# Agent attention and a maxout network in one kernel: one pool of PSUM banks, output products in two shapes, eleven more query groups turned by DMA, and a new order of all work

## The chip, the cores and the metric

The kernel runs on one core of a Trainium2 chip. Its time is the device time of one execution in microseconds (us); three runs of the kernel before gave 451.64, 454.34 and 454.73, median 454.34.

## The reference

Attention goes through 49 agents per batch; then each row passes a network whose hidden layer is the maximum of three products.

```python
B, N, C = (4, 12544, 128); n_agents = 49          # q, k, v: B x N x C, float32
def sm(a, b):                                      # softmax of scale * a @ b.T over b's rows
    ...
a2k = sm(agents, k)
agent_v = a2k @ v                                  # 49 x 128 per batch
q2a = sm(q, agents)
x = q2a @ agent_v                                  # 50176 rows of 128
h = max(max(x @ w1, x @ w2), x @ w3)               # 768 wide
out = h @ w_out                                    # 50176 x 128, float32
```

## The kernel before, in words

**Algebra.** Since x is q2a times a 49 x 128 matrix, the kernel multiplies the weights into that matrix once per batch (G, 49 agents by 1792 columns, kept twice, in partitions 0 to 48 and 64 to 112). With e the unnormalised exponentials of a query group, the hidden layer is e times parts of G. The maximum of three is written as w1 + max(0, w3 - w1, w2 - w1): two hidden products (u with the columns of w3 - w1, v with those of w2 - w1), a ReLU and a maximum, and a linear product for w1, which goes into the output bank directly (L582, out_linear). The row's sum divides at the very end.

**Stages.** Keys and values come in chunks of nine times 128 rows, cast to bf16. Batch 0 is done first: its chunks are transposed on PE (L342), scored (L359), exponentiated, summed (L370) and multiplied with the values (L376). Batches 1 to 3 follow beside the query work: their chunks are transposed by a DMA that SP issues (L454, tile KT<-KB).

**Query groups.** There are 49 groups s of 1024 rows, 12 per batch, and a last one with 256 rows of each batch. Per group: load, cast on POOL (L517), eight 128 x 128 transposes on PE into PSUM (L523) and a copy on DVE (L527), or, for groups 38 to 48 (TURNED), a DMA transposition from SP (L454, tile QT<-QB). Then scores (L533), exponentials on ACT (L539), sums (L545) and reciprocals (L550). The group's 1024 rows stand as two halves of 64 partitions side by side, so that each hidden product is a pair of matmuls of 49 rows and 512 columns in the two halves of the PE array (L558). For each of six blocks f of 128 hidden columns: u on PE, ReLU on ACT (L571), v on PE, maximum on DVE (L574) into the tile R; for f = 4 ACT does it in place and out of place (L565, L568) while v adds to u in PSUM. Output: 48 matmuls of R with w_out (L592, out_hidden) and four linear ones (L582), 0.5 group per output bank, each bank scaled by the reciprocals on DVE (L599) and the group stored.

**Forms on PE.** PE works in three forms: all 128 rows; two row halves (the hidden products); two column halves (scores, G). 

**PSUM.** Eight banks: three fixed pairs (UV, for u, v and the wide tiles) and two single banks (OM, for outputs, scores, sums and turned queries).

**Order.** All instructions of all engines stand in one hand-written list (ORDER); a name in it is one step of the function graph, and the number behind the slash is the slot that its new tile takes. The framework sets the waits by the tiles that are read and written. On each engine, and in SP's DMA queue, work runs strictly in this order. `Plan.add` holds a cost with each step; nothing in the kernel reads it.

Of the kernel before, what the change touches and what calls it, by code (L numbers as in the profile page):

```python
# [9 lines left out]
FP32 = mybir.dt.float32  # L10
# [7 lines left out]
DFF = NF * P  # L18
SCALE = 1.0 / math.sqrt(C)
C31, C21, C1O, WC = 0, DFF, 2 * DFF, 2 * DFF + 2 * C  # L20
CV, CS, CT = KT * A, KT * A + A, (KT - 1) * A
# [4 lines left out]
TURNED = range(38, 49)  # L26
# [5 lines left out]
SLOTS = {"UV": 3, "OM": 2, "LD": 13, "QB": 3, "KB": 3, "VB": 4, "KT": 3, "QT": 3, "EQ": 4, "EK": 4, "AS": 3,  # L32
         "R": 13, "RC": 4, "OS": 9, "G": 4, "VA": 2, "EA": 2, "ES": 2, "KR": 2}
SHAPE = {"UV": ([P, 2, 512], FP32), "OM": ([P, 512], FP32), "LD": ([P, KT, C], FP32), "QB": ([P, GT, C], BF16),
# [6 lines left out]
class Plan:  # L41


    def __init__(self):
        self.ops, self.index, self.tiles, self.maker = [], {}, {}, {}

    def add(self, name, eng, fn, cost, mode=FULL, after=(), new=(), use=(), bank=None, serve=0.0):
        self.index[name] = len(self.ops)
        for cls, t in new:
            self.tiles[t] = cls  # L50
            self.maker[t] = name
        seq = [self.maker[t] for t in use if self.maker[t] not in after]
        self.ops.append(dict(name=name, eng=eng, fn=fn, pace=cost[0], lat=cost[1], mode=mode, after=list(after), seq=seq,
                             new=[t for _, t in new], use=[t for _, t in new] + list(use), bank=bank, serve=serve))

    def places(self, order, given):

        left = {}
        for o in self.ops:
            for t in o["use"]:  # L60
                left[t] = left.get(t, 0) + 1
        free = {c: list(range(n)) for c, n in SLOTS.items()}
        place = {}
        for name in order:
            o = self.ops[self.index[name]]
            for i, t in enumerate(o["new"]):
                slots = free[self.tiles[t]]
                place[t] = slots.pop(slots.index(given[name][i]) if name in given else 0)
            for t in o["use"]:
                left[t] -= 1  # L70
                if left[t] == 0:
                    free[self.tiles[t]].append(place[t])
        return place

# [20 lines left out]
def mm(n, cols):  # L95
    t = n * max(cols / 2400 + 0.0025, 0.0253)
    return t, t + 0.235
# [18 lines left out]
def graph(plan, em):  # L116
# [3 lines left out]
    add("prep", PE, em.prep, (0.3, 3.6))  # L120
    ch = chunks(0)
    for g, (t0, n) in enumerate(ch):
# [4 lines left out]
        add(f"kt0.{g}", PE, em.k_turn(g, n), mm(n, 128), after=[f"kc0.{g}", "prep"], new=[("UV", f"kT_ps0.{g}")], use=[f"kb0.{g}"])  # L127
        add(f"ke0.{g}", DVE, em.k_evacuate(g, n), dve_half(n * 128), after=[f"kt0.{g}"], new=[("KT", f"kT0.{g}")], use=[f"kT_ps0.{g}"])
        add(f"ks0.{g}", PE, em.k_scores(0, g, n, f"s0.{g}"), mm(n, 49), after=[f"ke0.{g}"], new=[("UV", f"s0.{g}")], use=[f"kT0.{g}"])
        add(f"kx0.{g}", ACT, em.k_exps(0, g, n, f"s0.{g}"), (n * 0.041 + 0.07, n * 0.041 + 0.2), after=[f"ks0.{g}"],  # L130
            new=[("EK", f"e0.{g}")], use=[f"s0.{g}"])
        add(f"to0.{g}", PE, em.totals(g, n), mm(1, n * 49), after=[f"kx0.{g}"], new=[("OM", "acc")] if g == 0 else [],
            use=[f"e0.{g}"] + (["acc"] if g else []))
# [8 lines left out]
    for g in range(SPARE):  # L142
        add(f"wm.{g}", PE, em.warm(g), (0.2225, 0.45), new=[("UV", f"warm.{g}")])
# [12 lines left out]
    add("tw1", PE, em.turn_w1, mm(NF, 128), after=["cw1", "prep"], new=[("OM", "tw1")])  # L156
    add("ew1", DVE, em.evacuate_w1, dve_half(DFF), after=["tw1"], use=["tw1"])
    add("cwo", POOL, em.cast_wo, (0.77, 0.85), after=["lwo"], use=["wo"])
    add("rc0", DVE, em.recip_first, (0.85, 0.97), after=[f"to0.{g}" for g in range(last + 1)], new=[("KR", "kr0")], use=["acc"])
# [3 lines left out]
    for name, c, d, eng in (("a", C31, ["d31a"], ACT), ("b", C31 + half, ["d31b", "d32"], DVE), ("c", C21, ["d21a"], ACT),  # L163
                            ("d", C21 + half, ["d21b"], DVE)):
        add(f"gp{name}", PE, em.product(0, c, c + half, f"gp{name}"), mm(1, half), mode=COL, after=["nr0"] + d, new=[("UV", f"gp{name}")])
        add(f"gv{name}", eng, em.product_out(0, c, c + half, c, f"gp{name}", eng), act(half) if eng == ACT else dve(half),
            after=[f"gp{name}"], use=[f"gp{name}", "G0"])
    add("pl", PE, em.prep_linear, mm(NF, 128), after=["ew1", "cwo"], new=[("OM", "pl")])
    add("el", ACT, em.evacuate_linear, (0.17, 0.31), after=["pl"], use=["pl"])
    add("gl", PE, em.product(0, C1O, WC, "gl"), mm(1, 256), mode=COL, after=["nr0", "el"], new=[("OM", "gl")])  # L170
    add("gvl", ACT, em.product_out(0, C1O, WC, C1O, "gl", ACT), act(256), after=["gl"], use=["gl", "G0"])


    hosting = set()
    for b in range(1, B):
        ch = chunks(b)
        for g, (t0, n) in enumerate(ch):
            r, m = f"{b}.{g}", f"m.{host_of(b, g)}"
            hosting.add(host_of(b, g))
# [7 lines left out]
            add(f"ks{r}", PE, em.k_scores(b, g, n, m), mm(n, 49), after=[f"kt{r}"], new=[("OM", m)], use=[f"kT{r}"], bank=m)  # L187
            add(f"kx{r}", ACT, em.k_exps(b, g, n, m), (n * 0.041 + 0.07, n * 0.041 + 0.2), after=[f"ks{r}"], new=[("EK", f"e{r}")],
                use=[m], bank=m)
            add(f"kv{r}", PE, em.values(b, g, n, m), mm(n, 49), after=[f"kx{r}", f"vc{r}"], use=[m, f"vb{r}", f"e{r}"], bank=m)  # L190
            add(f"va{r}", DVE, em.add_values(b, g, m), (0.13, 0.25), after=[f"kv{r}"] + ([f"va{b}.{g - 1}"] if g else []),
                new=[] if g else [("VA", f"va{b}")], use=[m] + ([f"va{b}"] if g else []), bank=m)
            if g < len(ch) - 1:
                add(f"ea{r}", POOL, em.add_exps(b, g), (0.97, 1.06), after=[f"kx{r}"] + ([f"ea{b}.{g - 1}"] if g else []),
                    new=[] if g else [("EA", f"ea{b}")], use=[f"e{r}"] + ([f"ea{b}"] if g else []))
        g = len(ch) - 1
        add(f"fo{b}", POOL, em.fold(b), (1.25, 1.35), after=[f"ea{b}.{g - 1}"], new=[("ES", f"es{b}")], use=[f"ea{b}"])
        add(f"to{b}", PE, em.total(b, g, n, m), (n * 0.0253 + 0.1, n * 0.0253 + 0.335), after=[f"fo{b}", f"kv{r}"],
            use=[m, f"es{b}", f"e{r}"], bank=m)
        add(f"nr{b}", DVE, em.normalise(b, m), (0.5, 0.62), after=[f"to{b}", f"va{r}"], new=[("KR", f"kr{b}"), ("G", f"G{b}")],  # L200
            use=[m, f"va{b}"], bank=m)
        for name, c0, c1, eng in (("a", C31, C31 + DFF, ACT), ("c", C21, C21 + DFF, DVE), ("l", C1O, WC, ACT)):
            w = c1 - c0
            add(f"gp{name}{b}", PE, em.product(b, c0, c1, f"gp{name}{b}"), mm(1, w), mode=COL, after=[f"nr{b}", "el"],
                new=[("UV" if w > 512 else "OM", f"gp{name}{b}")])
# [4 lines left out]
    for s in range(NQ):  # L210
        parts = parts_of(s)
# [6 lines left out]
        else:  # L218
            add(f"qt.{s}", PE, em.q_turn(s), mm(GT, 128), after=[f"qc.{s}", "prep"], new=[("OM", f"qT_ps.{s}")], use=[f"qb.{s}"])
            add(f"qe.{s}", DVE, em.q_evacuate(s), (0.636, 0.735), after=[f"qt.{s}"], new=[("QT", f"qT.{s}")], use=[f"qT_ps.{s}"])  # L220
        add(f"sc.{s}", PE, em.q_scores(s), mm(len(parts), 512 // len(parts)), mode=COL, after=[f"qd.{s}" if s in TURNED else f"qe.{s}"],
            new=[("OM", f"qs.{s}")], use=[f"qT.{s}"])
        add(f"ex.{s}", ACT, em.q_exps(s), (0.56, 0.65), after=[f"sc.{s}"], new=[("EQ", f"e.{s}")], use=[f"qs.{s}"])
        m = f"m.{s}"
        h = s in hosting
        add(f"su.{s}", PE, em.sums(s, m, not h), mm(GT // 2, 2), after=[f"ex.{s}"] + ([f"ks{b}.{g}" for b in range(1, B)
            for g in range(len(LATER)) if host_of(b, g) == s] if h else []), new=[] if h else [("OM", m)], use=[f"e.{s}"] + ([m] if h else []),
            bank=m)
        add(f"re.{s}", DVE, em.recips(s, m), (0.13, 0.25), after=[f"su.{s}"], new=[("RC", f"rc.{s}")], use=[m], bank=m)
        for f in range(NF):  # L230
            def needs(base, first, second):
# [29 lines left out]
class Emit:  # L261
    def __init__(self, nc, pools, io):
# [10 lines left out]
        for t in self.avT:  # L273
            nc.vector.memset(t, 0.0)
# [590 lines left out]
```

## Time and profile before

| | us |
|---|---|
| median of three runs | 454.34 (451.64 to 454.73) |
| profiled execution, span from first to last instruction | 449.8 |
| PE busy (weight loads beside it) | 423.7 (274.0) |
| DVE busy | 402.8 |
| ACT busy | 395.1 |
| POOL busy | 169.4 |
| DMA moved | 117.8 MB |

Of the profiled execution the span is what is given; the runs' times hold what lies around it, too. Busy times are unions of the instructions' spans. On PE they include the pipeline's depth, so that matmuls overlap in the trace, and a price of one is better read from start to start. A line L558 is a line of the kernel; the two sides of `<-` are the tiles that it writes and reads. PEld is the weight load, SPq the issuing of DMAs by SP.

### The profile page before, as it was taken

The numbers are of one execution on the slowest core, as the hardware profiler recorded it, in microseconds if no ns is written. First come the engines' busy times: TensorE is split into PE (matmuls) and PEld (weight loads), VectorE is DVE, ScalarE is ACT, GpSimd is POOL, SyncE is SP. The second block draws the span as 40 slices with busy tenths as digits, with TensorE's granted clock in tenths as the row PEclk, the third lists the DMA queues.
The fourth block names the chain that finished last, engine by engine and source line by source line (L and its number), as shares of the span: only waits on it lengthen the run. The fifth ranks groups of instructions, "written<-read, shape, count | busy, mean of one in ns | idle before, by whom it ended". The sixth has DMA issues, their size and how long they took to land.

```text
span 449.8 us, 13103 instructions
## 1 busy us (share of the span) xinstructions
PE 423.7 (94%) x5388; PEld 274.0 (61%) x5388; DVE 402.8 (90%) x512; ACT 395.1 (88%) x461; POOL 169.4 (38%) x176
## 2 busy tenths in 40 slices
PE   0778899999999999999999999999999999999996
PEld 0654466666665666666666666666666655565675
DVE  1335999999999999999999999999999999999986
ACT  1459999999988999999989999999889899999983
POOL 1641645455676372464363263453402110100000
PEclk9989999999999999999999999999999999999999
DMA  8999999999999998999969799498608685327142
GB/s 311 409 408 387 326 373 310 263 394 316 340 320 274 392 216 223 408 273 318 406 200 324 216 350 226 141 314 336 212 6 230 191 221 129 96 103 178 48 177 107
DMA packets 80150, 117.80 MB, mean 262 GB/s; under 512 B 53527, under 2 KB 56283, under 8 KB 80091
## 3 DMA queue, kind: packets, MB, share of 16 engines
q1 hardware_dynamic: 79888, 116.87, 83.6%
q8 instruction: 42, 0.69, 0.6%
q14 instruction: 17, 0.14, 0.1%
q10 hardware_dynamic: 203, 0.10, 0.1%
HBM read 78.74 MB, written 25.69 MB: 232 GB/s over the span
## 4 chain that ended last, share of the span: by engine, by line
PE 73%; DMA 12%; DVE 6%; POOL 2%; ACT 2%; SPq 2%; issue 2%; POOLq 0%; DVEq 0%
PE UV L558 29%; PE OM L592 27%; DMA LD<-in_k_dram 6%; PE OM L582 5%; DMA LD<-in_v_dram 4%; DVE R L574 4%; PE OM L523 3%; PE OM L533 3%; PE OM L376 2%; DMA out_dram<-OS 2%; PE OM L359 2%; DVE OS L599 1%; SPq L454 1%; ACT AS L571 1%; ACT VB L333 1%
## 5 line engine op out<-in xcount | busy, mean ns | idle before, releaser
L574 DVE TENSOR_TENSOR R<-UV,AS 128x1024 bf16<-128x1024 f32 x245 | 293.4, 1219 | 11.4 <-PE UV L558 5.3
L571 ACT ACTIVATE AS<-UV 128x1024 bf16<-128x1024 f32 x245 | 246.7, 1023 | 18.3 <-PE UV L558 11.7
L558 PE MATMUL UV<-EQ,G 49*128 49x512 bf16 (+1 forms) x1248 | 178.5, 368 | 2.1 <-DVE R L574 1.3
L592 PE MATMUL OM<-wo_bf,R 128*128 128x128 bf16 x2352 | 179.8, 219 | 0.0
L592 PEld LDWEIGHTS <-R 128*128 128x128 bf16 x2352 | 139.7, 98 | 39.5 <-issue 37.3
L558 PEld LDWEIGHTS <-G 49*128 49x128 bf16 x1248 | 58.7, 93 | 63.9 <-issue 23.8
L517 POOL CAST QB<-LD 128x1024 bf16<-128x1024 f32 x49 | 50.8, 1040 | 111.9 <-DMA LD<-in_q_dram 50.6
L599 DVE TENSOR_TENSOR OS<-OM,RC 128x512 f32<-128x512 f32 x98 | 67.3, 686 | 2.6 <-PE OM L592 1.4
L335 POOL CAST KB<-LD 128x1152 bf16<-128x1152 f32 (+2 forms) x45 | 49.7, 1116 | 40.6 <-DMA LD<-in_k_dram 35.9
L335 POOL CAST VB<-LD 128x1152 bf16<-128x1152 f32 (+1 forms) x33 | 37.3, 1137 | 40.4 <-DMA LD<-in_v_dram 24.3
L568 ACT ACTIVATE R<-UV 128x1024 bf16<-128x1024 f32 x49 | 50.1, 1022 | 2.5 <-PE UV L558 1.7
L565 ACT ACTIVATE UV<-UV 128x1024 f32<-128x1024 f32 x49 | 49.9, 1019 | 2.3 <-DVE R L574 1.2
L582 PE MATMUL OM<-G,EQ 128*128 128x256 bf16 x196 | 37.9, 275 | 0.0
L474 POOL TENSOR_TENSOR EA<-EA,EK 128x441 f32<-128x441 f32 x27 | 27.6, 1023 | 18.5 <-ACT EK L365 18.1
L539 ACT ACTIVATE EQ<-OM 128x512 bf16<-128x512 f32 x49 | 29.4, 601 | 1.0 <-PE OM L533 0.9
L527 DVE COPY QT<-OM 128x1024 bf16<-128x1024 bf16 x38 | 26.0, 684 | 1.1 <-PE OM L523 1.0
L347 DVE COPY KT<-UV 128x1152 bf16<-128x1152 bf16 (+1 forms) x12 | 8.2, 700 | 18.2 <-PE UV L342 18.2
L523 PE MATMUL OM<-ident,QB 128*128 128x128 bf16 x304 | 23.7, 222 | 0.6 <-POOL QB L517 0.6
L582 PEld LDWEIGHTS <-EQ 128*128 128x128 bf16 x196 | 12.3, 97 | 15.9 <-issue 15.2
L523 PEld LDWEIGHTS <-QB 128*128 128x128 bf16 x304 | 18.5, 99 | 4.3 <-issue 2.6
L359 PEld LDWEIGHTS <-KT 128*128 128x128 bf16 x392 | 14.3, 98 | 10.0 <-issue 5.5
L533 PE MATMUL OM<-QT,agT 128*64 128x512 bf16 (+1 forms) x104 | 20.2, 393 | 0.0
(67 smaller groups left out, 196.4 us busy)
## 6 DMA issues: line engine op xcount, KB each, us to landing
LD<-in_q_dram SPq DMA_DIRECT2D x48, 512.0 KB, 6.6
out_dram<-OS SPq DMA_DIRECT2D x48, 512.0 KB, 6.3
LD<-in_k_dram SPq DMA_DIRECT2D x40, 576.0 KB, 7.8
LD<-in_v_dram SPq DMA_DIRECT2D x40, 576.0 KB, 9.4
LD<-in_k_dram SPq DMA_DIRECT2D x3, 512.0 KB, 6.0
LD<-in_v_dram SPq DMA_DIRECT2D x3, 512.0 KB, 11.4
LD<-in_moe_w_dram SPq DMA_DIRECT2D x6, 192.0 KB, 8.4
KT<-KB SPq DMA_TRANSPOSE x33, 6.7
```

The costliest lines, as they stand in the source:

```text
L335: (self.nc.gpsimd if eng == POOL else self.nc.vector).tensor_copy(out=out, in_=src)
L517: return lambda: self.nc.gpsimd.tensor_copy(out=self.t[f"qb.{s}"], in_=self.t[f"q.{s}"][:, :GT, :])
L523: self.nc.tensor.transpose(t[:, j * P:(j + 1) * P], self.t[f"qb.{s}"][:, j, :], self.ident)
L533: self.nc.tensor.matmul(self.t[f"qs.{s}"][h * H:(h + 1) * H, jj * P:(jj + pairs) * P], self.agT[:, b, :], self.t[f"qT.{s}"][:, 2 * jj + h: ...
L558: self.nc.tensor.matmul(t[:, h, jj * P:(jj + pairs) * P], self.t[f"G{b}"][h * H:h * H + A, c + f * P:c + (f + 1) * P], self.t[f"e.{s}"][h ...
L565: return lambda: self.nc.scalar.activation(self.t[f"u.{s}.{f}"], self.t[f"u.{s}.{f}"], AF.Relu)
L568: return lambda: self.nc.scalar.activation(self.t[f"r.{s}.{f}"], self.t[f"u.{s}.{f}"], AF.Relu)
L571: return lambda: self.nc.scalar.activation(self.t[f"a.{s}.{f}"], self.t[f"u.{s}.{f}"], AF.Relu)
L574: return lambda: self.nc.vector.tensor_tensor(out=self.t[f"r.{s}.{f}"], in0=self.t[f"v.{s}.{f}"], in1=self.t[f"a.{s}.{f}"], op=ALU.max)
L582: self.nc.tensor.matmul(self.t[f"o.{s}.{o}"][:, i * 2 * C:(i + 1) * 2 * C], self.t[f"e.{s}"][:, jj * P:(jj + 1) * P], self.t[f"G{of[jj]}"] ...
L592: self.nc.tensor.matmul(self.t[f"o.{s}.{o}"][:, c:c + C], self.t[f"r.{s}.{f}"][:, h, jj * P:(jj + 1) * P], self.wo_bf[:, f, :], start=Fals ...
L599: self.nc.vector.tensor_tensor(out=self.t[f"os.{s}"][:, j:j + 4, :], in0=self.t[f"o.{s}.{o}"].rearrange("p (j c) -> p j c", c=C), in1=self ...
```

## The change

1. **PSUM.** One pool of eight banks (PS). u, v and the wide tiles take two neighbouring banks, all else one, any that the list names.
2. **Linear product** (out_linear): each group's four matmuls of 128 rows and 256 columns become eight of 49 rows and 128 columns, in pairs in the two row halves, one bank each. G loses its second, zero-filled half of columns (WC).
3. **Output products** by place: where the table ROWS has an r, a block's products (out_halves) are 16 matmuls of 64 rows in pairs instead of 8 of 128 rows; both output banks of the group then fill together. The bank o now holds the rows of half o, not those of the first or second half of the column blocks, and the scaling writes every other block of the output tile.
4. **Sides.** The first of a block's two steps has rows 0 to 63 write bank 0 and rows 64 to 127 bank 1, the second the other way round. A step that follows one of the other kind in the same banks waits until PE has finished that one.
5. **TURNED** has 22, 25, 28 and 30 to 37 in addition to 38 to 48.
6. **Set-up.** The identity, ones and agents become steps of the list. G of batches 1 to 3 is made in five pieces of at most 384 columns in place of three. Normalising is two steps, folding four, and the sums have a bank of their own.
7. **Waits.** The kernel sets its own semaphores (Plan.waits) inside one critical section of the framework. A helper issues all instructions, so every row has line L379.
8. **Order.** The list is another one throughout.

```diff
-C31, C21, C1O, WC = 0, DFF, 2 * DFF, 2 * DFF + 2 * C
+C31, C21, C1O, WC = 0, DFF, 2 * DFF, 2 * DFF + C
-TURNED = range(38, 49)
+TURNED = (22, 25, 28, *range(30, 49))
+ROWS = """
+ffffff ffffff fffrfr ffffrf ffffff rfffrf ffffff rfffrr ffffrf ffffff ffffff ffffff rfrfrr ffffff frfffr ffffff ffffff rrffff
...
-SLOTS = {"UV": 3, "OM": 2, "LD": 13, "QB": 3, "KB": 3, "VB": 4, "KT": 3, "QT": 3, "EQ": 4, "EK": 4, "AS": 3,
+SLOTS = {"PS": 8, "LD": 13, "QB": 3, "KB": 3, "VB": 4, "KT": 3, "QT": 3, "EQ": 4, "EK": 4, "AS": 3,
...
+                if t in o["sides"]:
+                    was = side.get(t)
+                    if was and was[0] != o["sides"][t]:
+                        forced.add(was[1])
+                    side[t] = (o["sides"][t], name)
...
-    def out_linear(self, s, o):
+    def out_linear(self, s):
         def fn():
             of = [p[0] for p in parts_of(s) for _ in range(p[4])]
-            for i in range(2):
-                jj = 2 * o + i
-                self.nc.tensor.matmul(self.t[f"o.{s}.{o}"][:, i * 2 * C:(i + 1) * 2 * C], self.t[f"e.{s}"][:, jj * P:(jj + 1) * P],
-                                      self.t[f"G{of[jj]}"][:, C1O:C1O + 2 * C], start=(i == 0), stop=False, skip_group_check=True)
+            for jj in range(GT // 2):
+                for h in range(2):
+                    rows = slice(h * H, h * H + A)
+                    self.nc.tensor.matmul(self.t[f"o.{s}.{h}"][:, jj * C:(jj + 1) * C], self.t[f"e.{s}"][rows, jj * P:(jj + 1) * P],
+                                          self.t[f"G{of[jj]}"][rows, C1O:], start=self.opens(s, h) and jj == 0, stop=True,
+                                          skip_group_check=True)
...
+    def out_halves(self, s, o, f):
+        def fn():
+            for jj in range(GT // 2):
+                for k in range(2):
+                    rows, h = slice(k * H, (k + 1) * H), k ^ o
+                    self.nc.tensor.matmul(self.t[f"o.{s}.{h}"][:, jj * C:(jj + 1) * C], self.t[f"r.{s}.{f}"][rows, h, jj * P:(jj + 1) * P],
+                                          self.wo_bf[rows, f, :], start=self.opens(s, h) and jj == 0, stop=True, skip_group_check=True)
```

How this moves the work, at three places.

PE, around the linear product of group 22. Before (a weight load and a matmul are rows of their own; EQ holds e, R the maxima):

```order
L558 LDWEIGHTS G_2626
L558 MATMUL UV_4741<-EQ_4654,G_2626 128x512
...
L582 LDWEIGHTS EQ_4460
L582 MATMUL OM_4746<-G_2626,EQ_4460 128x256
...
L592 LDWEIGHTS R_4620
L592 MATMUL OM_4746<-wo_bf,R_4620 128x128
...
L558 LDWEIGHTS G_2626
L558 MATMUL UV_4759<-EQ_4460,G_2626 128x512
```

PE, the same linear product in the new order (x8 of R is one step of 64-row pairs, x4 one of 128 rows):

```order
L379 MATMUL ps<-EQ_109,G_145 128x512 x2
L379 MATMUL ps<-G_145,EQ_108 128x128 x8
L379 MATMUL ps<-EQ_109,G_145 128x512 x2
L379 MATMUL ps<-wo_bf,R_122 128x128 x8
L379 MATMUL ps<-EQ_109,G_145 128x512 x2
L379 MATMUL ps<-wo_bf,R_122 128x128 x8
L379 MATMUL ps<-wo_bf,R_128 128x128 x4
```

Linear and output products in 64-row pairs now stand between hidden products without a change of form; the next 128-row step changes it.

SP, where the last key chunks of batch 3 are turned, before:

```order
L454 DMA_TRANSPOSE KT_5775<-KB_5748 128x9x128
L325 DMA LD_5807<-in_k_dram 128x1024
L513 DMA LD_5814<-in_q_dram 128x1024
L513 DMA LD_5823<-in_q_dram 128x1024
L325 DMA LD_5835<-in_v_dram 128x1152
L454 DMA_TRANSPOSE KT_5847<-KB_5649 128x9x128
```

SP, the same stretch of the new order:

```order
L379 DMA_TRANSPOSE KT_102<-KB_94 128x9x128
L379 DMA LD_89<-in_q_dram 128x1024
L379 DMA LD_87<-in_q_dram 128x1024
L379 DMA_TRANSPOSE QT_106<-QB_93 128x8x128
L379 DMA LD_83<-in_k_dram 128x1152
L379 DMA_TRANSPOSE QT_105<-QB_92 128x8x128
L379 DMA LD_86<-in_q_dram 128x1024
```

Transpositions of query groups now stand between those of the keys; up to the last key transposition there are eight of them, before there were none.

DVE, up to the first maximum (R) of group 0, before (wall holds the weights' differences, w1T the turned w1):

```order
L448 CAST G_646<-UV_662 128x384
L398 TENSOR_TENSOR wall<-LD_453,LD_416 128x384
L413 COPY w1T<-OM_670 128x768
L448 CAST G_646<-UV_686 128x384
L550 RECIPROCAL RC_705<-OM_531 128x8
L527 COPY QT_714<-OM_696 128x1024
L574 TENSOR_TENSOR R_726<-UV_709,AS_677 128x1024
```

DVE, the same in the new order:

```order
L379 COPY w1T<-ps 128x768
L379 CAST G_144<-ps 128x384
L379 TENSOR_TENSOR wall<-LD_79,LD_87 128x384
L379 TENSOR_TENSOR R_130<-ps,AS_116 128x1024
L379 COPY QT_106<-ps 128x1024
L379 CAST G_144<-ps 128x384
```

The second copy of G and the copy of the turned group now stand behind the first maximum.

852 lines of the change are left out of this document (495 added, 357 removed).

## The prediction

> **What bounds the kernel now.** I read the page's totals first, then a table by stage, then one period of the steady part instruction by instruction.
>
> ```profile
> span 449.8 us, 13103 instructions
> PE 423.7 (94%) x5388; PEld 274.0 (61%) x5388; DVE 402.8 (90%) x512; ACT 395.1 (88%) x461; POOL 169.4 (38%) x176
> DMA  8999999999999998999969799498608685327142
> PE 73%; DMA 12%; DVE 6%; POOL 2%; ACT 2%; SPq 2%; issue 2%; POOLq 0%; DVEq 0%
> ```
>
> Three engines are near 90%, and the chain that ended last runs through PE for 73% of the span. By stage (columns: PE, PEld, DVE, ACT, POOL busy with their counts, clock, DMA share, GB/s):
>
> ```profile
> 50.00:100.00 50.00, 49.53 (x647) 32.29 (x646) 47.31 (x61) 47.19 (x57) 27.09 (x26) 1.00 1.07 335
> 100.00:150.00 50.00, 48.77 (x631) 31.17 (x629) 47.76 (x61) 45.16 (x54) 30.75 (x33) 1.00 1.10 322
> 200.00:250.00 50.00, 49.92 (x652) 32.66 (x650) 48.89 (x63) 46.88 (x56) 23.21 (x25) 1.00 0.91 300
> 350.00:400.00 50.00, 49.69 (x517) 28.38 (x516) 48.25 (x52) 48.02 (x54) 6.21 (x6) 1.00 0.52 139
> ```
>
> Busy PE proves little, since matmuls overlap; what counts is whether one starts when the one before lets it. The PE timeline of one period (one query group) shows that:
>
> ```profile
> 202.72 0.82 PE L558 MATMUL UV<-EQ,G 49*128 49x512 bf16 x6
> 203.48 0.39 PE L582 MATMUL OM<-G,EQ 128*128 128x256 bf16 x2
> 203.71 0.61 PE L523 MATMUL OM<-ident,QB 128*128 128x128 bf16 x8
> 204.15 0.61 PE L592 MATMUL OM<-wo_bf,R 128*128 128x128 bf16 x8
> 204.70 0.84 PE L558 MATMUL UV<-EQ,G 49*128 49x512 bf16 x6
> 205.47 1.07 PE L592 MATMUL OM<-wo_bf,R 128*128 128x128 bf16 x16
> 206.46 0.41 PE L533 MATMUL OM<-QT,agT 128*64 128x512 bf16 x2
> 206.80 0.82 PE L558 MATMUL UV<-EQ,G 49*128 49x512 bf16 x6
> 207.56 0.39 PE L582 MATMUL OM<-G,EQ 128*128 128x256 bf16 x2
> 207.78 0.61 PE L592 MATMUL OM<-wo_bf,R 128*128 128x128 bf16 x8
> 208.23 0.39 PE L359 MATMUL OM<-agT,KT 128*128 128x49 bf16 x9
> 208.46 0.24 PE L545 MATMUL OM<-sel,EQ 128*128 128x2 bf16 x4
> 208.63 0.60 PE L558 MATMUL UV<-EQ,G 49*128 49x512 bf16 x4
> 209.17 0.40 PE L592 MATMUL OM<-wo_bf,R 128*128 128x128 bf16 x4
> 209.40 0.39 PE L376 MATMUL OM<-EK,VB 128*128 128x49 bf16 x9
> 209.73 0.39 PE L558 MATMUL UV<-EQ,G 49*128 49x512 bf16 x2
> 210.05 0.84 PE L592 MATMUL OM<-wo_bf,R 128*128 128x128 bf16 x12
> 210.84 0.82 PE L558 MATMUL UV<-EQ,G 49*128 49x512 bf16 x6
> ```
>
> Start to start gives prices. Eight products without a change of form (207.78 to 208.23) take 0.45, 0.056 each; eight followed by 49-row work (204.15 to 204.70) take 0.55. So a change of form (128 rows, two 49-row halves, or two column halves) costs 0.10; 16 products plus a change take 0.99, which says 0.09. I use 0.095. A pair of 49-row matmuls takes 0.226 (0.54 for two pairs plus a change, 0.76 for three), a linear one of 256 columns 0.11. The period of 8.12 (202.72 to 210.84) is then 12 pairs 2.71, 48 products 2.69, four linear 0.44, turning 0.44, scores 0.24, sums 0.10, keys and values 0.46, and 11 changes 1.05: 8.13. Nothing is left over: **PE does not wait here; it is the bound**, and an eighth of its time goes to changes of form. DVE is next:
>
> ```profile
> 204.58 0.68 DVE L527 COPY QT<-OM 128x1024 bf16<-128x1024 bf16 x1
> 207.30 3.49 DVE L574 TENSOR_TENSOR R<-UV,AS 128x1024 bf16<-128x1024 f32 x3
> 210.71 0.20 DVE L465 TENSOR_TENSOR VA<-OM,VA 128x49 f32<-128x49 f32 x1
> 210.82 0.20 DVE L550 RECIPROCAL RC<-OM 128x8 f32<-128x8 f32 x1
> 210.94 0.69 DVE L599 TENSOR_TENSOR OS<-OM,RC 128x512 f32<-128x512 f32 x1
> 211.56 1.22 DVE L574 TENSOR_TENSOR R<-UV,AS 128x1024 bf16<-128x1024 f32 x1
> ```
>
> Three maxima take 3.41 to the next start, 1.137 each; a scaling 0.62; the copy 0.61 (its 0.68 less the 0.07 by which neighbours overlap); the small ones 0.12 and 0.11. A group costs DVE 5 x 1.137 + 2 x 0.62 + 0.61 + 0.23 = 7.77, so it idles 0.35 of 8.12.
>
> **The change part by part.**
>
> Linear products. Four matmuls of 0.11 per group become eight of 49 rows and 128 columns, in pairs. The last query group, whose four batches each bring 128 columns, shows that shape in its hidden products:
>
> ```profile
> 437.91 0.84 PE L558 MATMUL UV<-EQ,G 49*128 49x128 bf16 x24
> 438.69 0.39 PE L582 MATMUL OM<-G,EQ 128*128 128x256 bf16 x2
> ```
>
> Twelve pairs take 0.78 with a change, (0.78 - 0.095)/12 = 0.057: a pair costs what one full product does. So 0.44 becomes 0.22: 49 x 0.22 = **10.6 less**.
>
> Output products as 64-row pairs. 158 of the 588 are issued so (two for each r of the table ROWS): four pairs of 0.056 for four products of 0.056, nothing by itself. What it saves is changes of form. Counted along the two orders, PE changes form 569 times before and 492 after: 77 x 0.095 = **7.3 less**.
>
> Turning. Eleven more groups (22, 25, 28 and 30 to 37) lose eight PE products (11 x 0.44 = **4.9 less**) and one DVE copy (11 x 0.61 = **6.7 less on DVE**), and gain a DMA transposition.
>
> Waits of PE on itself. Where products of the other half follow into the same two banks, PE waits for its own earlier work; the order has 56 such places, 49 of them with one group of 0.22 between.
>
> ```profile
> L592 PE MATMUL OM<-wo_bf,R 128*128 128x128 bf16 x2352 | 179.8, 219 | 0.0
> ```
>
> Such a matmul shows 0.22 from start to end, so the group between covers most of it. Between 0 and 0.3 each (a whole group and a change): I take 0.05, near the covered end, **2.8 more**. The Trainium skill ("TensorEngine Tiling (Array Packing)", Gotcha 1: PSUM Pressure) says that different row tiles may not be in one bank at once and that software has to keep them apart, which is what these waits are for. For a group's signal the Trainium skill ("TensorE: Matmul & The Clock Gate", The cost: per-tile semaphore tail) has a tail of 25 + 4.7 per tile + 26.3 per signal ns; for eight tiles and one signal that is an estimate of 0.09 a wait, with which the sum would be 2.2 later. No row here shows such a wait.
>
> Pooled banks, G in five pieces, own semaphores. In the period above PE never waits for a bank, so the pool by itself gains nothing there. The pieces add one DVE copy to each of three batches, under 3 x 0.62 and more likely a tenth of it. In the new order's rows no weight load stands by itself, so a wait ahead of a group holds its load too. That is free while PE comes late, and costs a fraction of a change of form, 0 to 0.1, where PE comes early; I put it with what is given back.
>
> The start. DMA of the first 14 MB sets it, and these bytes stay. But the first maximum comes late behind the first hidden product:
>
> ```profile
> 42.00 0.39 PE L558 MATMUL UV<-EQ,G 49*128 49x512 bf16 x2
> 45.48 1.22 DVE L574 TENSOR_TENSOR R<-UV,AS 128x1024 bf16<-128x1024 f32 x1
> ```
>
> In the new order the second copy of G, a reciprocal and the copy of a turned group (0.61 by the row above) come behind the first maximum and not ahead of it. Of 3.5 I take **1.5 less** (0 to 2.5).
>
> Given back. PE's price falls by 10.6 + 7.3 + 4.9 - 2.8 = 20.0, or 0.41 a group; DVE's by 6.7, 0.14 a group. If all came out, DVE's idle 0.35 would shrink to 0.08, 1% of a period, while ACT stays as full as it is. Two engines at their limit wait for each other: in the stage from 350, where hardly a group is turned on PE or copied on DVE, DVE still has 1.75 of 50 idle in the row above. I leave it 0.18 a group, so **5 come back** (0 if PE's whole gain comes out, 13.3 if DVE keeps all its idle time).
>
> The DMA. It must stay hidden under all this. From 50 to 150 it was full: 32.9 MB (335 and 322 GB/s) with 14 transpositions of 0.29 MB among them.
>
> ```profile
> L454 SPq DMA_TRANSPOSE KT<-KB x14: 1233/3775/8161, 51.9 to 148.0; - x14
> L454 SPq DMA_TRANSPOSE KT<-KB x33: 1233/2805/8161, 46.8 to 315.1; - x33
> 15.00:30.00 15.00, 11.42 (x173) 8.95 (x173) 6.81 (x11) 8.67 (x13) 8.48 (x9) 1.00 1.03 408
> ```
>
> Plain loads alone ran at 408 GB/s, so the other 28.8 MB took 70.6, and a transposition (100 - 70.6)/14 = 2.1. Up to the last key transposition SP's order holds 88.6 MB and 33 transpositions, 286 us of DMA in 315 (91%); the new order holds 86.5 MB and 41 of them, eight of these with eight blocks for nine, 296, and comes there one group earlier, near 298: **full all the way**, where the old order let up behind 150. What a full DMA costs is in the stage table: PE's busy time is 0.39 and 1.15 below the 49.92 of a stage that is not full, 0.8 on the mean. Three more such stages are **2.4 more** (0 if the loads come in time, and the rival below if not).
>
> Sum: 449.8 - 20.0 - 1.5 + 5 + 2.4 = 435.7. That is the span of the one profiled execution; the median of the runs is 454.34, 4.5 above it, so **440.2**.
>
> **The rivals.**
>
> DVE keeps its idle time: PE's gain turns into waiting for maxima. For it speaks DVE's 96% in the period; against it, that its idle time there has no cause but PE. Time 454.3 - 6.7 = 447.6.
>
> All of it comes out, and nothing is given back: 454.3 - 20.0 - 1.5 = 432.8, and 429 with free self-waits and the better start. For it: PE itself ran with nothing left over at 8.12.
>
> Handed back on PE: the 56 self-waits cost 0.3 each, 16.8 instead of 2.8, while PE is still the bound: 440.2 + 14 = 454.2, no change. Against it: 0.22 of work lies between.
>
> Slower: **the DMA becomes the bound.** Eight query transpositions now come ahead of the last keys, SP issues in order, and PE's order waits for each key chunk. If the DMA is kept only as busy as before, 91%, its 296 take 325. Behind that place stand 449.8 - 315.1 = 134.7, one group of 8.1 more, and 17 groups that are 0.3 shorter, 137.7: span 463, time 467. It decides from below 93% on, where the time passes 459. For it: nearly 100% is asked for over 300 us. Against it: the page shows the DMA at eight tenths or more through the first 19 slices, and PE still had 49 of each 50 us.
>
> The change doesn't do what it says, if pairs of 64-row products did not run side by side: the last group shows that they do, so it gets no chance of its own.
>
> **How the numbers follow.** The forecast (431 to 447) has 0.57, all comes out 0.10, DVE keeps its idle 0.13, handed back 0.11, DMA 0.09. A change of 1%, 4.5 us, is about what a measurement can tell from none. Faster: the first three, since the third ends 6.7 below, 0.80. Same: handed back, 0.11. Slower: the DMA, 0.09. The range runs from 428, where everything comes out, to 454, where the self-waits hand it back; beyond lie the DMA case and the tails.
>
> **What would show it.** Right: PE periods with 64-row work beside the 49-row work and no 0.095 between; groups 0 to 21 near 8.0, groups 36 to 48 near 7.3; DVE busy over 97% of each stage; the last key transposition near 298. Wrong: PE idle ahead of the keys' products with DMA as releaser (DMA); PE idle between products of two halves of a group (self-waits); the pairs 0.11 apart; or DVE idle as before while PE idles too, which would say that the coupling and not PE's price set the period.

## The result, and the profile after

The changed kernel takes 446.39 us (median of four runs, 445.11 to 448.74) beside 453.16 of the kernel before (four runs): a ratio of 0.987 with a 95% interval of 0.982 to 0.992 (the two medians alone give 0.985). It is 1.3% faster, where 3.1% was forecast. One of the four executions of b_pe, a kernel of below, took 879 us and stands outside its ratio. The page of the changed kernel's profiled execution, lines that answer to those of before:

```profile
span 444.1 us, 14119 instructions
PE 413.0 (93%) x6128; PEld 258.4 (58%) x6128; DVE 393.5 (89%) x502; ACT 391.4 (88%) x464; POOL 170.2 (38%) x177
DMA  8999999999999999999999999999979445556333
PE 65%; DMA 10%; DVE 9%; ACT 5%; POOL 5%; issue 4%; SPq 1%; POOLq 0%; DVEq 0%; ACTq 0%
```

PE's share of the chain fell from 73% to 65%, those of DVE (6 to 9), ACT and POOL (2 to 5 each) grew, and the DMA is at eight tenths or more through the first 29 slices. The table by stage (columns as before):

```profile
50.00:100.00 50.00, 49.96 (x729) 31.49 (x727) 48.02 (x61) 46.34 (x57) 28.45 (x28) 1.00 1.06 320
100.00:150.00 50.00, 49.71 (x711) 31.12 (x709) 47.76 (x64) 46.06 (x57) 27.23 (x30) 1.00 1.10 334
200.00:250.00 50.00, 48.51 (x729) 30.63 (x727) 46.48 (x60) 45.45 (x55) 23.27 (x26) 1.00 1.07 339
350.00:400.00 50.00, 49.25 (x761) 29.42 (x754) 48.15 (x56) 48.38 (x54) 5.21 (x5) 1.00 0.45 99
```

DVE is at 93 to 96% of each stage, not over 97%. PE does what the change says. Its timeline, late in the kernel:

```profile
416.77 0.39 PE L379 MATMUL ps<-EQ,G 49*128 49x512 bf16 x2
417.00 0.61 PE L379 MATMUL ps<-wo_bf,R 64*128 64x128 bf16 x16
417.44 0.39 PE L379 MATMUL ps<-EQ,G 49*128 49x512 bf16 x2
417.67 0.40 PE L379 MATMUL ps<-wo_bf,R 64*128 64x128 bf16 x8
417.91 0.39 PE L379 MATMUL ps<-EQ,G 49*128 49x512 bf16 x2
418.13 0.39 PE L379 MATMUL ps<-G,EQ 49*128 49x128 bf16 x8
418.36 0.39 PE L379 MATMUL ps<-EQ,G 49*128 49x512 bf16 x2
```

Start to start a step of 64-row products takes 0.22 (two of them 0.44), the linear product 0.23 (418.13 to 418.36), and no change of form stands between. The group at 417.67 is one that waits for PE's own work, the second of the two steps at 417.00, with one hidden pair between: it starts 0.23 behind that pair.

Where did the time come from? I cut both executions at the first maximum of groups 0, 22 and 30 and at the end of the last maximum (the columns are those of the table by stage). Before, then after:

```profile
45.48:230.18 184.70, 181.62 (x2370) 117.95 (x2369) 177.29 (x225) 171.78 (x203) 101.89 (x104) 1.00 1.05 315
230.18:296.21 66.03, 65.95 (x858) 42.89 (x856) 64.32 (x81) 62.53 (x74) 29.03 (x29) 1.00 0.88 260
296.21:444.34 148.13, 147.58 (x1782) 92.80 (x1781) 142.89 (x164) 137.57 (x154) 22.77 (x25) 1.00 0.54 164
```

```profile
43.18:229.50 186.32, 182.28 (x2596) 113.01 (x2596) 175.88 (x226) 171.27 (x204) 102.31 (x103) 1.00 1.07 318
229.50:294.37 64.87, 64.25 (x936) 39.23 (x936) 61.86 (x78) 61.99 (x76) 28.70 (x28) 1.00 1.12 310
294.37:437.38 143.01, 140.52 (x2232) 86.92 (x2231) 137.35 (x160) 136.56 (x156) 24.42 (x27) 1.00 0.65 168
```

The start gained 2.3 (45.48 to 43.18), the first 22 groups lost 1.6, the next eight gained 1.2, the last 19 gained 5.1, and from the last maximum to the end it takes 1.3 longer (5.5, now 6.7): 5.7 in all. PE's price (every start in both traces at the unhindered price of its kind) fell by 22.7: its matmuls from 348.0 to 332.6 and its changes of form from 53.4 to 46.1. So PE got all its relief and gave most of it back as waiting. About 17 of the 22.7 lie in the last 27 groups (75 changes of form, 7.1; ten groups not turned on PE, 4.4; 27 linear products, 5.9), and these gained 6.3 (66.03 + 148.13 to 64.87 + 143.01). The waits by engine (total, times, longest), before and after:

```profile
ACT AS L571 <- PE UV L558: 11.7, 38, 0.8
DVE R L574 <- PE UV L558: 5.3, 17, 0.6
PE UV L558 <- DVE R L574: 1.3, 3, 0.8
```

```profile
PEld ps L379 <- DVE R L379: 22.8, 87, 0.5
PEld ps L379 <- ACT AS L379: 16.0, 58, 0.8
ACT AS L379 <- PE ps L379: 12.4, 34, 0.6
DVE R L379 <- PE ps L379: 9.4, 27, 0.9
```

After the change PE's weight loads wait for DVE's maxima and ACT's ReLUs to leave a bank, and DVE in turn waits more for PE (9.4 against 5.3), although PE has less to do. The rows of PEld have no counterpart before: there the matmul held the wait and not its load (last row of before), and a load that waits can still have PE's earlier matmuls running beside it. So 22.8 is not what PE lost.

### The profile page after: what moved, and what is told of

It is laid out like the page before. It is cut to its first block, busy times and chain, and to the rows that moved or that the text cites. A ratio compares the mean times of both kernels' runs of the same rounds, so it can differ in the third digit from the quotient of the medians.

```text
span 444.1 us, 14119 instructions
## 1 busy us (share of the span) xinstructions
PE 413.0 (93%) x6128; PEld 258.4 (58%) x6128; DVE 393.5 (89%) x502; ACT 391.4 (88%) x464; POOL 170.2 (38%) x177
## 4 chain that ended last, share of the span: by engine, by line
PE 65%; DMA 10%; DVE 9%; ACT 5%; POOL 5%; issue 4%; SPq 1%; POOLq 0%; DVEq 0%; ACTq 0%
PE ps L379 65%; DVE R L379 6%; ACT AS L379 4%; DMA LD<-in_q_dram 3%; DMA out_dram<-OS 2%; DVE OS L379 2%; DMA KT<-KB 2%; DMA LD<-in_v_dram 2%; DMA LD<-in_k_dram 1%; POOL QB L379 1%; POOL VB L379 1%; SPq L379 1%; POOL EA L379 1%; POOL KB L379 1%; ACT R L379 1%
## 5 line engine op out<-in xcount | busy, mean ns | idle before, releaser
L379 DVE TENSOR_TENSOR R<-ps,AS 128x1024 bf16<-128x1024 f32 x245 | 293.9, 1219 | 13.9 <-PE ps L379 9.4
L379 ACT ACTIVATE AS<-ps 128x1024 bf16<-128x1024 f32 x245 | 245.3, 1029 | 16.2 <-PE ps L379 12.4
L379 PE MATMUL ps<-EQ,G 49*128 49x512 bf16 (+1 forms) x1248 | 196.6, 370 | 3.6 <-DVE OS L379 0.5
L379 PE MATMUL ps<-wo_bf,R 128*128 128x128 bf16 (+1 forms) x2984 | 187.4, 218 | 1.0 <-issue 0.8
L379 PEld LDWEIGHTS ps<-wo_bf,R 128*128 128x128 bf16 (+1 forms) x2984 | 137.1, 96 | 57.2 <-issue 37.3
L379 PEld LDWEIGHTS ps<-EQ,G 49*128 49x128 bf16 x1248 | 55.5, 93 | 70.2 <-DVE R L379 21.3
L379 POOL CAST QB<-LD 128x1024 bf16<-128x1024 f32 x49 | 51.3, 1050 | 106.3 <-DMA LD<-in_q_dram 53.0
L379 POOL CAST KB<-LD 128x1152 bf16<-128x1152 f32 (+2 forms) x45 | 50.0, 1119 | 59.4 <-DMA LD<-in_k_dram 36.3
L379 DVE TENSOR_TENSOR OS<-ps,RC 128x512 f32<-128x512 f32 x98 | 66.5, 680 | 2.9 <-DMA out_dram<-OS 1.7
L379 ACT ACTIVATE R<-ps 128x1024 bf16<-128x1024 f32 x49 | 50.2, 1025 | 2.1 <-PE ps L379 1.8
L379 ACT ACTIVATE ps<-ps 128x1024 f32<-128x1024 f32 x49 | 50.0, 1020 | 1.8 <-PE ps L379 1.2
L379 POOL CAST VB<-LD 128x1152 bf16<-128x1152 f32 (+1 forms) x33 | 37.3, 1139 | 33.0 <-DMA LD<-in_v_dram 28.5
L379 POOL TENSOR_TENSOR EA<-EA,EK 128x441 f32<-128x441 f32 x27 | 27.7, 1024 | 13.6 <-ACT EK L379 13.2
L379 ACT ACTIVATE EQ<-ps 128x512 bf16<-128x512 f32 x49 | 29.5, 601 | 2.3 <-PE ps L379 1.9
L379 ACT ACTIVATE EK<-ps 128x441 bf16<-128x441 f32 (+2 forms) x45 | 23.8, 533 | 4.4 <-PE ps L379 4.2
L379 ACT ACTIVATE VB<-LD 128x1152 bf16<-128x1152 f32 (+1 forms) x12 | 12.3, 1051 | 17.1 <-DMA LD<-in_v_dram 14.0
L379 PE MATMUL ps<-agT,KT 128*128 128x49 bf16 x392 | 17.4, 185 | 5.7 <-DVE KT L379 3.3
L379 DVE COPY QT<-ps 128x1024 bf16<-128x1024 bf16 x27 | 18.4, 681 | 3.2 <-PE ps L379 3.1
L379 PE MATMUL ps<-QT,agT 128*64 128x512 bf16 (+1 forms) x104 | 19.9, 388 | 0.0
L379 PEld LDWEIGHTS ps<-agT,KT 128*128 128x128 bf16 x392 | 14.3, 97 | 9.0 <-DVE KT L379 4.0
L379 PE MATMUL ps<-G,EQ 49*128 49x128 bf16 x392 | 19.1, 217 | 0.0
L379 DVE COPY KT<-ps 128x1152 bf16<-128x1152 bf16 (+1 forms) x12 | 8.2, 699 | 12.0 <-PE ps L379 12.0
```

The costliest lines, as they stand in the source:

```text
L379: i = call(*args, **named)
```

## The experiments

My first theory was that PE's price had stopped being the limit and that DVE, with the banks that it gives back, had become it. Its rivals: PE's price still sets the time, or the full DMA does. Ratios are to the kernel before, run beside them on the same chip. 1% is 4.5 us, and the intervals are near plus or minus 2 us. The changed kernel itself stands at 0.987 and 0.989 in two measurements, so at 0.988 below.

**One engine lighter at a time (a_pe, a_dve, a_act).** Edits, in this order:

```diff
-            for jj in range(GT // 2):
+            for jj in range(GT // 2 - (f < 4)):                       # out_hidden and out_halves
```
```diff
-        ... out=self.part(f"r.{s}.{f}", half), in0=self.t[v], in1=self.part(f"a.{s}.{f}", half), op=ALU.max)
+        ... out=self.part(f"r.{s}.{f}", half)[..., :W], in0=self.t[v][..., :W], in1=self.part(f"a.{s}.{f}", half)[..., :W], op=ALU.max)
```
```diff
-        return lambda: self.nc.scalar.activation(self.part(out, half), self.t[name], AF.Relu)
+        w = W if out.startswith("a.") else 512                        # W = 464
+        return lambda: self.nc.scalar.activation(self.part(out, half)[..., :w], self.t[name][..., :w], AF.Relu)
```

> The changed kernel with a lighter PE: blocks 0 to 3 leave out the output products of the last quarter of the columns, so a group has 8 products of 0.056 less, 0.45, 22 us in all; everything else stays (a quarter of the output lacks these blocks). If PE's price still sets the time, as the prediction held, a group becomes as cheap as DVE allows (about 7.6 where it now takes 8.04) and the time falls by 12 to 18. If DVE, ACT and the eight banks set it together and PE only waits for banks, most of the 22 turns into more waiting for banks: 2 to 6 less. If the full DMA sets it: less than 2.

> The changed kernel with a lighter DVE: the maxima take 464 of each 512 columns, 96 of 1024 less or 0.1 each, five per group, 24 us in all; the last quarter's products read the last 128 columns that are there, so PE's work is the same (the columns left out lack their maxima). If PE's price sets the time: 0 to 2 less. If DVE and the banks that it gives back set it: 8 to 15 less, since each bank pair also comes free 0.1 sooner. If the DMA: less than 2.

> The changed kernel with a lighter ACT: the ReLUs of five blocks take 464 of each 512 columns, 0.08 less each, 0.4 a group, 20 us in all (the columns left out hold zeros, set once at the start). PE's price: 0 to 2 less. ACT and the banks of u as part of the limit: 4 to 10 less. DMA: less than 2.

Measured: a_pe 0.981 (0.975 to 0.987), a_dve 0.984 (0.979 to 0.989), a_act 0.982 (0.978 to 0.986): 2 to 3 us each of 20 to 24 that were taken away. That is what "PE's price" foretold for DVE, and what "DVE and the banks" foretold for PE. Both theories fell: no engine alone is the limit. The intervals are as wide as these gains; the traces tell more. The last 27 groups, 207.88 in the changed kernel, of a_pe, a_dve, a_act (columns as before):

```profile
231.00:436.56 205.56, 199.34 (x2864) 114.91 (x2863) 198.55 (x237) 198.33 (x231) 52.28 (x54) 1.00 0.75 210
228.71:434.30 205.59, 202.01 (x3162) 125.07 (x3161) 190.01 (x237) 197.47 (x231) 53.11 (x54) 1.00 0.79 215
229.09:434.83 205.74, 202.87 (x3164) 125.85 (x3162) 198.51 (x237) 190.46 (x231) 53.04 (x54) 1.00 0.80 215
```

Each brings 2.1 to 2.3 there.

**Less for the DMA (a_store, a_load).**

```diff
-                self.nc.sync.dma_start(self.io["out"][r, :].rearrange("(p j) c -> p j c", j=n), self.t[f"os.{s}"][:, cut, :])
+                self.nc.sync.dma_start(self.io["out"][r, :].rearrange("(p j) c -> p j c", j=n)[:, :n // 2, :],
+                                       self.t[f"os.{s}"][:, cut.start:cut.start + n // 2, :])
```
```diff
-            self.nc.sync.dma_start(self.t[f"{which}{b}.{g}"][:, :n, :], src)
+            m = n // 2 if b and (which, b, g) != ("v", 1, 2) else n
+            self.nc.sync.dma_start(self.t[f"{which}{b}.{g}"][:, :m, :], src[:, :m, :])     # q_load alike, from group 3 on
```

> The changed kernel with half of each store left out (half of the output is not written): 12.8 of 120.8 MB less for the DMA, about a tenth of its load; no engine's work changes. If the full DMA holds the kernel up: 8 or more less. If PE, or DVE with the banks: at most 3 less, which would be the two stalls of 1.3 us that PE shows ahead of key scores.

> The changed kernel with half of the bytes of nearly all query loads and of the key and value loads of batches 1 to 3 left out (the rest of each tile holds older data): 31 of 120.8 MB less; transpositions and stores stay, no engine's work changes. If the DMA's load sets the first thirty groups: these fall from 251 by 10 or more. If the engines do: at most 4 less, the late key chunks and the late store.

Measured: a_store 0.982 (0.978 to 0.985), a_load 0.979 (0.976 to 0.982), 3 and 4 us less. Where, the three parts of a_load show:

```profile
43.11:225.62 182.51, 181.52 (x2596) 113.33 (x2595) 175.76 (x225) 170.46 (x204) 101.44 (x103) 1.00 0.75 203
225.62:290.50 64.88, 64.26 (x936) 39.23 (x937) 61.84 (x79) 62.00 (x76) 29.25 (x29) 1.00 0.83 204
290.50:433.32 142.82, 140.49 (x2232) 86.89 (x2231) 137.34 (x160) 136.55 (x156) 22.99 (x25) 1.00 0.52 142
```

All of it lies in the first 22 groups (186.3 to 182.5); behind them a lighter DMA changes nothing (64.87 and 64.88, 143.0 and 142.8). The expectation had put 4 less with the engines and 10 or more with the DMA; the place of the gain says DMA, and so do the ends of these 22 groups. The first maximum of group 22 comes at 228.7 to 231.0 in a_pe, a_dve, a_act and the changed kernel (229.5), at 227.6 in a_store and at 225.6 in a_load.

**Several engines at once (a_all, a_pedve), and with the loads (a_allload).** The three edits of above together; PE and DVE without ACT; and a_all with a_load. (Lines of these kernels are L380.)

> The changed kernel with PE, DVE and ACT lighter at once (0.45, 0.5 and 0.4 a group, by the same pieces left out of blocks 0 to 4 as in the three single runs); loads, stores, transpositions and POOL stay. If the three engines hold each other (each alone at 95% of its stage, so that one alone gained nothing), all three together free the period: from 8.04 to about 7.6, 15 to 20 less, in the first thirty groups as in the last. If the DMA, full until 300 us, sets the first thirty groups: those stay at 251 and only the last nineteen gain, 6 to 9 less.

> PE and DVE lighter as in a_all, ACT with all its work. If ACT is as much a limit as the other two, most of the gain is lost again: 3 to 6 less than the changed kernel. If PE and DVE are the pair that sets the period: 9 to 12 less, as with all three.

> All three engines lighter as in a_all, and half of the load bytes left out as in a_load. If the DMA holds the first 22 groups once the engines are lighter: they fall from 187 to 174 to 178 and the time to 421 to 426. If something else does (POOL, the keys' chain through ACT and PE): they stay above 183 and the time near 430, which is a_all's less the 4 that the loads were worth.

Measured: a_all 0.959 (0.954 to 0.963), 13 less; a_pedve 0.973 (0.970 to 0.977), 7 less; a_allload 0.934 (0.931 to 0.937), 24 less. The first two lie between the ranges expected, the third within its own. The parts of a_all, then of a_allload:

```profile
42.80:229.68 186.88, 177.54 (x2411) 105.60 (x2410) 166.98 (x225) 162.71 (x204) 102.91 (x104) 0.97 1.07 322
229.68:291.46 61.78, 60.97 (x861) 35.69 (x861) 58.27 (x78) 59.09 (x76) 28.83 (x29) 1.00 1.09 318
291.46:425.55 134.09, 132.24 (x2005) 78.18 (x2005) 128.45 (x160) 128.89 (x156) 23.55 (x26) 1.00 0.66 176
```

```profile
43.62:219.03 175.41, 173.81 (x2409) 104.49 (x2410) 166.21 (x225) 161.61 (x203) 101.31 (x103) 0.99 0.81 207
219.03:280.80 61.77, 60.97 (x861) 35.71 (x862) 58.29 (x78) 59.07 (x76) 29.20 (x29) 1.00 0.81 221
280.80:414.86 134.06, 132.20 (x2005) 78.19 (x2005) 128.43 (x160) 129.00 (x156) 22.94 (x25) 1.00 0.57 151
```

This settles the last 27 groups. All three lighter by 0.4 to 0.5 a group bring 12.0 there (64.9 + 143.0 to 61.8 + 134.1), 0.44 a group: the whole. Each engine alone brings about a fifth (rows above), PE and DVE together 5.8, half. PE with ACT, and DVE with ACT, were not run. In the first 22 the three bring nothing (186.9 against 186.3) until the loads are cut too; then 11.5 (to 175.4). So the three engines hold one another, and in the first 22 groups the DMA stands in front of that. How it reaches the engines can be seen in a_all. At 203.59 SP issues a store behind seven loads that it had issued since 197.3. A scaling of group 19, whose output tile that store has to leave, can start 10.6 later (the median store of the changed kernel lands after 5.8). It waits 4.0 (1.7 in the changed kernel), and PE behind it 3.46:

```profile
203.59 0.44 SPq L380 DMA_DIRECT2D out_dram<-OS  x1
214.21 0.69 DVE L380 TENSOR_TENSOR OS<-ps,RC 128x512 f32<-128x512 f32 x1 [3.98 <-DMA out_dram<-OS]
214.96 0.40 PE L380 MATMUL ps<-agT,KT 128*128 128x49 bf16 x9 [3.46 <-DVE OS L380]
215.41:222.24 6.83, 6.83 (x58) 3.60 (x56) 4.82 (x7) 3.21 (x5) 4.62 (x6) 0.50 1.20 280
```

The last row is the stretch right behind, in the columns of the table by stage: PE's granted clock is 0.50 for 6.83 us. Another wait of PE, 1.53 at 98.2 for a transposed key chunk, is followed by 3.41 us at 0.50. The two waits are 5.0, and 10.2 us at half the clock cost up to 5.1 more: together up to 10.1 of the 11.5 that lighter loads bring. a_pe has the same wait, 3.36, and 7.1 us at 0.50 within its first 22 groups. Its execution with the highest mean clock (0.989; the others 0.974 to 0.981) took 439.3, the others 444 to 445. So its 3 us may well understate what a lighter PE is worth at the full clock. Whether the full DMA would cost a_all as much without the wait for this one store, no run shows (m_two, below, takes it out of the changed kernel only).

**Parts of the change undone (c_lin, c_full, c_linfull, c_turn).** Of c_linfull, which joins the first two:

```diff
-                                          self.t[f"G{of[jj]}"][rows, C1O:], ...
+                                          self.t[f"G{of[jj]}"][:, C1O + h * C:C1O + (h + 1) * C], ...   # c_lin
     place = plan.places(order, given)
+    ROWS[:] = ["ffffff"] * 49                                                                       # c_full
+    plan = Plan()
+    graph(plan, em)
```
```diff
-TURNED = (22, 25, 28, *range(30, 49))
+TURNED = (22, *range(38, 49))                    # c_turn; ten words qd.N of the list become qt.N and qe.N
```

> The changed kernel with the linear product in its old form alone: eight matmuls of 128 rows and 128 columns (G again with zero halves), same place in the order. PE's price rises by 49 x 0.22 = 10.8, and its changes of form from 492 to 559, 67 x 0.095 = 6.4: 17.2. If PE's price sets the time: 13 to 17 more. If PE has 25 us of waiting for banks in it that can take up such work: 5 to 10 more.

> The changed kernel with all output products in the 128-row form, same places and order: no 64-row pairs, no waits of PE on itself between them, and 676 changes of form where there were 492, 184 x 0.095 = 17.5 more for PE. PE's price: 13 to 18 more. PE with waiting in it that takes up work: 5 to 10 more.

> The changed kernel with the linear product and all output products in their old forms: what is left of the change is the pool of banks, the eleven groups turned by DMA and the order. PE's price rises by 10.8 and by 211 changes of form, 20.0: 30.8, which is 8 above that of the kernel before. PE's price: 27 to 31 more, above the kernel before. If the waiting for banks takes up work: 15 to 22 more.

> The changed kernel with ten of the eleven groups (25, 28, 30 to 37) turned on PE again and copied by DVE, put into gaps of the list in which a bank is free: PE 10 x 0.44 + 12 changes of form x 0.095 = 5.5 more, DVE 6.1 more, ten transpositions by DMA less. If either PE's or DVE's price sets the time: 5 to 7 more. If the DMA sets it: 5 or more less. If neither is at its limit: within 2.

Measured: c_lin 1.013 (1.011 to 1.015), c_full 1.011 (1.007 to 1.015), c_linfull 1.036 (1.034 to 1.037), that is 11, 10 and 21 more for 17.2, 17.5 and 30.8 of PE's price, between or within the two ranges expected. About two thirds of what PE gets more comes out as time. In the last 27 groups, at the full clock, it is about three quarters (c_lin 7.8, c_full 9.9, of some 10 and 14), against the fifth of what PE gets less (a_pe). c_linfull is 16 slower than the kernel before with only 8 more of PE's price and less work for DVE: in this list the pool, the turning and the order bring nothing without the short forms. c_turn, 1.029 (1.027 to 1.031) or 18 more, does not answer its question. PE waits for the bank at each of the places that I chose, such as

```profile
261.42 0.62 PE L379 MATMUL ps<-ident,QB 128*128 128x128 bf16 x8 [1.34 <-DVE R L379]
334.84 0.62 PE L379 MATMUL ps<-ident,QB 128*128 128x128 bf16 x8 [1.48 <-DVE R L379]
```

and ten such waits of 0.5 to 1.5 come to 11.5, more than the 5.5 of work that was moved. What turning alone is worth stays open.

**The two longest waits (m_two, against the changed kernel, again).** PE waits 1.17 ahead of key scores at 216.68 for a scaling that waits for a store, and as long at 161.6 for a transposed key chunk.

```diff
-ov.19.0/3 ... ov.20.0/8 ... ov.28.0/8 ... v.14.1/1,2 ks2.3/7 kv2.2 p.13.0.5 ... v.14.0/5,6 ...
+ov.19.0/8 ... ov.20.0/3 ... ov.28.0/3 ... v.14.1/1,2 kv2.2 p.13.0.5 ... v.14.0/5,6 ks2.3/7 ...
```

> The changed kernel itself once more, as the measure for the next one: 446 beside 452 to 453 of the kernel before, ratio 0.987.

> The changed kernel without its two longest waits of PE: the output tile of group 19 takes a slot whose store left long ago (19 and 20 exchange their slots, and 28 follows), and the scores of key chunk 3 of batch 2 come three steps later on PE. If these two stalls, 1.24 and 1.34, are what the full DMA costs: 2 to 2.6 less than the changed kernel. If the DMA only comes late elsewhere then: within 1 of it.

Measured: 447.03 against 446.88, ratios 0.990 (0.987 to 0.994) and 0.989 (0.986 to 0.993): no gain. Such waits wander. In the second execution of the unchanged list (first row) neither of the two stands where it stood, and there is one of 1.62 elsewhere; in m_two's (second row) another of 0.76:

```profile
104.69 0.40 PE L379 MATMUL ps<-agT,KT 128*128 128x49 bf16 x9 [1.62 <-DMA KT<-KB]
```
```profile
175.39 0.39 PE L379 MATMUL ps<-EK,VB 128*128 128x49 bf16 x9 [0.76 <-ACT AS L379]
```

**The kernel before, lighter (b_pe, b_dve).** The edits of a_pe and a_dve in its functions.

```diff
-                for h in range(2):
+                for h in range(2 - (i == 1 and f < 4)):               # b_pe
```
```diff
-        ... out=self.t[f"r.{s}.{f}"], in0=self.t[f"v.{s}.{f}"], in1=self.t[f"a.{s}.{f}"], ...
+        ... out=self.t[f"r.{s}.{f}"][:, :, :W], in0=self.t[f"v.{s}.{f}"][:, :, :W], in1=self.t[f"a.{s}.{f}"][:, :, :W], ...   # b_dve
```

> The kernel before with a lighter PE: blocks 0 to 3 leave out one of four output products, 8 of 0.056 per group, 22 us in all. If PE is the bound there, as the prediction read it (price 8.13 of a period of 8.12, DVE idle 0.35 a group): 12 to 15 less, up to DVE's limit. If DVE keeps its idle time whatever PE costs, as the changed kernel's first thirty groups suggest: 2 to 5 less.

> The kernel before with a lighter DVE: maxima over 464 of 512 columns, 0.5 a group, 24 us in all, with PE's work the same. If PE alone is the bound: within 2 of the kernel before. If DVE and PE hold each other: 3 to 8 less.

Measured: b_pe 0.983 (0.979 to 0.988), 7.5 less; b_dve 0.996 (0.994 to 0.999), 1.7 less. So PE was tighter than DVE before the change (ACT was not tried there), but a third of its relief came out and not two thirds. The first 22 groups of b_pe take 181.5 where they took 184.7: 3.2 for 9.9 of work; the last 27 take 211.7 where they took 214.2, a fifth as in a_pe. By its own expectation b_dve spoke for PE as the only bound, and b_pe against it.

## Why the prediction was wrong

The direction was right, and so were the prices of work on PE; the size was off by half. (49 x 0.22 is 10.8 and 11 x 0.44 is 4.8, not 10.6 and 4.9: 0.1 in the sum.) By its steps (us, on the profiled executions):

| step | forecast | measured |
|---|---|---|
| PE: linear products, changes of form, turning | -22.8 | -22.7 |
| PE's waits on itself | +2.8 | 0 to +0.5 |
| start | -1.5 | -2.3 |
| given back | +5 (0 to 13.3) | +14.2 (what is left) |
| DMA full | +2.4 more than before | +3.8 in all (half of the loads, a_load, first 22 groups) |
| behind the last maximum | none | +1.3 |
| sum | -14.1 | -5.7 |

The sums differ by 8.4; the last step, from span to median, was taken as 4.5 and is now 2.3, which leaves the 6.2 between 440.2 and 446.4. No run lightened the loads of the kernel before. How much of the 3.8 it paid already stays open, and what was given back would be larger by that. The start's 2.3 is in part chance: the first maximum comes at 42.2 to 46.3 in fourteen executions with the new list and at 44.5 to 45.5 in three with the old, 1.4 apart in the mean.

**The step that failed is "given back".** It left DVE 0.18 of idle time a group out of 0.35, on the ground that PE's price set the period and the others would follow until their own limit. Ahead of it stands the sentence "PE does not wait here; it is the bound". That was true of the one period it was read from and did not carry over: the kernel before pays 7.5 for 22 (b_pe). With PE, DVE and ACT at 92 to 99% of each of the three parts (rows above), each waits for the others in turn, eight banks between them, and a lighter one turns its gain into waiting. It shows where a lighter DMA changes nothing: of the about 17 that PE's price fell by in the last 27 groups, about 11 came back, and DVE's idle time there went from 0.26 to 0.32 a group, not to 0.18. The rival "DVE keeps its idle time", which I gave 0.13, has the better mechanism, though ACT belongs in it as much as DVE (a_pedve 7, a_all 13). That it nearly has the number (447.6 against 446.4) is luck: it let all of DVE's 6.7 come out, and of 24 less on DVE 1.7 and 2 came out (b_dve, a_dve). That the eight banks alone are the limit is not shown: from first write to last read they are held 87 to 91% of the time behind the first groups, and in a_dve, where this falls by up to 2 points, the time hardly moves; no run has another number of banks.

The Trainium skill ("Perfetto Trace Analysis", Identifying the Most-Contended Engine) names the engine with the highest occupancy as the one to optimize first, and for TensorE takes the busy share of the weight loads (or the share of peak FLOPs) and not that of the matmuls. By the loads that engine was DVE in the kernel before (90%, PEld 61%), and the runs do not agree: 24 less on DVE brought 1.7 (b_dve), 22 less on PE 7.5 (b_pe).

**Waits on itself** cost nothing: 56 places, and a hidden pair between covers all but 0.01 of each. The estimate of 0.09 from the Trainium skill ("TensorE: Matmul & The Clock Gate", The cost: per-tile semaphore tail) is not tested: 0.22 of other work lies between, and no run shows such a wait without it.

**A wait that holds its weight load too**, put at 0 to 0.1 each: a hidden pair behind another row-form step takes 0.216 at the least and mostly 0.22 to 0.23 start to start, with a wait and without. A held load that is not late shows no price above 0.01.

**The DMA** was judged rightly in that it is full all the way and costs a few us. The last key transposition starts at 303.5, between the forecast 298 and the 315.1 of before. What the forecast did not see is that the first 22 groups with a full DMA take only 2% more than with a lighter one (186.3 against 182.5), so that even a real gain on all engines would have stopped there, as a_all's did.

**Signs.** Groups 0 to 21 were to be near 8.0 and are at 8.47 (186.3 / 22); before, they were at 8.40 (184.7 / 22) and not at the 8.12 of the one period. Groups 36 to 48, near 7.3, are at 7.4. That is no proof of PE's price, since DVE's own price there is 5 x 1.137 + 2 x 0.62 + 0.11 = 7.04, and a lighter PE left that stage almost as it was (7.3).

## What to carry to other kernels

When several engines stand above 90% of a stage, price the relief of one as a fraction (here a fifth, in stages at the full clock), and ask what the others and the DMA would let through. The test is cheap: leave out an equal share of work on one engine at a time and then on all, and cut the execution by stage, since one period without a wait says nothing of the others. Look at the granted clock of each stage before pricing it. Adding work to PE cost about two thirds of its price here, though taking as much away brought little.

## What the runs showed of the hardware

From the end of a ReLU or maximum to the start of the matmul that waited for its bank it takes 0.055 to 0.058 us (medians), the weight load included (it begins at 0.051 to 0.053). Steps in row halves of 64 and of 49 rows follow each other (hidden, linear and output products, 417.00 to 418.36 above) at 0.22 to 0.23 each with no price between. Behind PE's waits of 1.53 us and more (a_all twice, a_pe, a_pedve, again; up to 4.87) the granted clock stood at 0.50 for 3.4 or 6.8 us; behind c_turn's, up to 1.48, it did not fall. And SP is held by the issue of a transposition, the longer the fuller the DMA:

```profile
L379 SPq DMA_TRANSPOSE KT<-KB x33: 1247/3070/8359, 46.6 to 303.5; - x33
```

That is 1.2 us at best, 3.1 in the median and 8.4 at worst (ns: least, median, most), during which no load or store behind it is issued. With half of the loads left out (a_load) the median is 1.4.
